# Top-k attention with a feed-forward behind it: weights converted in fewer VectorE operations between search rounds, feed-forward dealt evenly

## The chip, the cores and the metric

One core of a Trainium2 chip runs the whole program. Its engines, as the profile names them: PE (TensorE, matrix products; PEld is its weight load), DVE (VectorE), ACT (ScalarE), POOL (GpSimd) and SP (SyncE, which here only issues transfers); 16 DMA engines move data. The metric is device time in microseconds; lower is better.

## The reference

All inputs are 64-bit floats; the result is 32-bit.

```python
B, H, S, D = 8, 8, 576, 64            # q, k, v: (B, H, S, D)
scores = (1/sqrt(D)) * q @ k.T        # per b, h: 576 x 576
kth = the 32nd largest of each row
scores = where(scores >= kth, scores, -1e9)
attn = exp(scores - max); attn /= sum(attn) + 1e-9
x = (attn @ v) laid out as (B*S, H*D) = (4608, 512)
h = x @ w_in                          # w_in (512, 2048)
g = h - tanh(h)
out = g @ w_out                       # w_out (2048, 512)
```

q, k and v come in as 32-bit floats; w_in and w_out as 64-bit floats, which the kernel turns into 32-bit ones itself.

## The kernel before

**Steps.** The attention is cut into 144 steps: for each of the 8 batch entries 16 main steps (a pair of heads by one of four groups of 128 queries) and 2 remainder steps (64 queries of two pairs of heads), 18 in all. The main loop in `run` is software-pipelined: in its turn n it works on four steps at once. In the order of the code: `weigh(n-2)` (PE transposes of the weights `z` into `zt`, L325, copied out by ACT, L328), `mask(n-1)` (ACT L268, POOL L271), `search(n)` (DVE: the 32 largest of each row by rounds of MAX8 and MATCH_REPLACE8, L227 to L238), some feed-forward, `scores(n+1)` (PE L197, copied to `sc` by ACT L205), the last transpose of `weigh(n-2)` (L331, L332), `expo(n-1)` (ACT L284), feed-forward, `values(n-2)` in every second main step and in remainder steps (PE `av` L355, L363; ACT `xs` L367; POOL `xT` L377), the transposes and copies of q and k (`turn_kq`, L170 to L181) and the loads of a pair of heads, and feed-forward again. Every engine runs its instructions in this order. The scores lie in one PSUM tile (`sc_ps`, one buffer): `scores(n+1)` on PE waits until DVE's L227 and L228 of step n have read it.

**Feed-forward.** A unit is 256 rows of x; there are 18 (two for each batch entry, and one of remainders for every four entries). A unit is 32 items for PE: 16 `ffn_h` (eight matmul records each, L397; after every second one ACT takes tanh, L409, and a copy, L410, and POOL subtracts, L411) and 16 `ffn_o` (four records each, L417). When `values` finishes a unit its items go on the list `work`; `deal(part)` hands out `part` of 4.4 items per step, in three parts of a step (0.5, 0.25, 0.25), for as long as the list holds any. What is left behind the last step runs then.

**Weights.** `convert(j, i)` turns one of 32 pieces of 128 x 512 numbers into 32-bit floats. Its load of 512 KB is issued by SP (L110, tile `raw`). DVE takes the exponent field (L116), ACT scales it (L117), POOL clamps it (L124); DVE takes the upper fraction bits (L119) and adds the lower word (L120), ACT scales (L123); DVE sets the sign (L129), POOL multiplies fraction and power (L132). Turns -1 to 10 of the main loop carry three pieces each, written behind `search`.

The reciprocal of the row sums (`invert`, DVE L303) stands after the first search round of turn n for step n-2; POOL spreads it (L346, tile `rx`) inside `values`.

Of the kernel before, what the change touches and what calls it, by code (L numbers as in the profile page):

```python
# [12 lines left out]
U32 = mybir.dt.uint32  # L13

# [27 lines left out]
def kernel(  # L42
# [41 lines left out]
    hpool = pool("h", 2)  # L84
    thpool = pool("th", 3)
    gpool = pool("g", 6)
# [13 lines left out]
    NW = 512  # L100

    def convert(j, i):

        if j < WJ:
            src, dst = moe_w_in[i * P : (i + 1) * P, j * NW : (j + 1) * NW], w_in[j][:, i, :]
        else:
            r0 = ((j - WJ) * FJ + i) * P
            src, dst = moe_w_out[r0 : r0 + P, :], w_out[j - WJ][:, i, :]
        raw64 = gpool.tile([P, NW, 2], U32, tag="g", name="raw64")
        nc.sync.dma_start(raw64[:].rearrange("p n w -> p (n w)"), src.bitcast(U32))  # L110
        yield
        lo, hi = raw64[:, :, 0], raw64[:, :, 1]
        f = thpool.tile([P, NW], FP32, tag="th", name="f")
        fu = f[:].bitcast(U32)

        nc.vector.tensor_scalar(fu, hi, 20, 0x7FF, ALU.logical_shift_right, ALU.bitwise_and)  # L116
        nc.scalar.activation(f[:], fu, AF.Copy, bias=-896.0 * 2.0**23, scale=2.0**23)  # L117

        nc.vector.tensor_scalar(dst.bitcast(U32), hi, 0x000FFFFF, None, ALU.bitwise_and)  # L119
        nc.vector.scalar_tensor_tensor(  # L120
            out=dst, in0=lo, scalar=2.0**-32, in1=dst.bitcast(U32), op0=ALU.mult, op1=ALU.add
        )
        nc.scalar.activation(dst, dst, AF.Copy, bias=1.0, scale=2.0**-20)  # L123
        nc.gpsimd.tensor_scalar(  # L124
            f[:].bitcast(I32), f[:], 0.0, 255.0 * 2.0**23, ALU.max, ALU.min
        )
        yield

        nc.vector.scalar_tensor_tensor(  # L129
            out=fu, in0=hi, scalar=0x80000000, in1=fu, op0=ALU.bitwise_and, op1=ALU.bitwise_or  # L130
        )
        nc.gpsimd.tensor_tensor(dst, dst, f[:], ALU.mult)  # L132
        yield
# [74 lines left out]
    def search(n, exact):  # L208
# [23 lines left out]
        for i in range(rounds):  # L232
            m8 = slice(8 * i, 8 * i + 8)
            for t in range(2):
                nc.vector.max(m[:, t, m8], last[t] if i == rounds - 1 else cur[t])  # L235
            if i < rounds - 1:
                for t in range(2):
                    nc.vector.match_replace(nxt[t], m[:, t, m8], cur[t], NEG)  # L238
                cur = nxt
            if i == 0:  # L240
                yield
# [57 lines left out]

    def invert(n):  # L300
        g, rd = steps[n], rds.get(n)
        if rd is not None and (g.rem or g.qt % 2):
            nc.vector.reciprocal(rd[:], rd[:])  # L303
# [32 lines left out]
    def values(n):  # L336
# [6 lines left out]
        rd = rds.pop(n)  # L343
        nq = 1 if g.rem else 2
        rx = xpool.tile([P, 2, 2, D], FP32, tag="rx", name="rx")
        nc.gpsimd.tensor_copy(rx[:, 0:nq], rd[:].unsqueeze(3).to_broadcast([P, nq, 2, D]))  # L346
# [19 lines left out]
        xs = xpool.tile([P, 2, N], FP32, tag="xs", name="xs")  # L366
# [46 lines left out]
    def ffn_o(u, i, part):  # L413
# [12 lines left out]
        ot = hpool.tile([P, DM], FP32, tag="ot", name="ot")  # L426
# [4 lines left out]
    def ffn(u):  # L431
        for f in range(CF):
            yield lambda f=f: ffn_h(u, f)
        for i in range(2):
            for part in range(CF // 2):
                yield lambda i=i, part=part: ffn_o(u, i, part)
# [28 lines left out]
    def run(exact):  # L465
        plan()
        NS = len(steps)
        items = len(rests) + len(units)
        share = 1.1 * items * 2 * CF / NS
# [6 lines left out]
        at(-6, lambda: load_kq(*pairs[0]))  # L476
        for i, (b, hp) in enumerate(pairs):
            n = first[b] + 2 * hp
            turn = turn_kq(b, hp)
            at(n - 4, lambda turn=turn: next(turn))  # L480
            at(n - 3, lambda turn=turn: next(turn))
            if i + 1 < len(pairs):
                at(n - 3, lambda i=i: load_kq(*pairs[i + 1]))
            at(n - 2, lambda b=b, hp=hp: load_v(b, hp))
        pieces = [] if exact else [convert(j, i) for j in range(2 * WJ) for i in range(FJ)]
        for i, piece in enumerate(pieces):
            for s in range(3):
                at((i + s) // 3 - 1, lambda piece=piece: next(piece))
        credit = 0.0

        def deal(part):
            nonlocal credit
            credit += part * share
            while work and credit > 0:
                work.pop(0)()
                credit -= 1
            credit = credit if work else min(credit, 0.0)

        for n in range(-6, NS + 2):
            here = lambda i: 0 <= n + i < NS  # L500
            if here(-2):
                w = weigh(n - 2)
                next(w)
            if here(-1):
                mask(n - 1, exact)
            if here(0):
                s = search(n, exact)
                next(s)
                if here(-2):
                    invert(n - 2)  # L510
                next(s, None)
            elif here(-2):
                invert(n - 2)
            deal(0.5)
# [6 lines left out]
            deal(0.25)  # L521
            if here(-2):
                values(n - 2)
            for fn in todo.pop(n, []):
                fn()
            deal(0.25)
        while work:
            work.pop(0)()
# [48 lines left out]
```

## Time and profile before

| | us |
|---|---|
| median of 3 runs | 1871.41 (1869.48 to 1871.91) |
| the profiled execution, its own time | 1873.38 |
| span of that execution, first to last instruction | 1871.6 |

| engine | busy us | share of the span |
|---|---|---|
| PE | 1645.2 | 88% |
| DVE | 1200.5 | 64% |
| ACT | 1066.4 | 57% |
| POOL | 954.0 | 51% |

Busy time is the time in which an engine had an instruction in hand. The shares are averages over a program with stages of different limits, so they are read by stretch. The tables by stretch give for each engine its busy time and in brackets its instructions, then the granted clock of TensorE (1.00 is 2.4 GHz, 0.50 is 1.2 GHz), the busy share of the DMA engines and GB/s. A row of the timeline is: start, duration, engine, line, operation, output<-inputs, count; in square brackets the idle time ahead of it and what ended it.

### The profile page before, as it was taken

The page shows a single profiled execution, that of the slowest core. Times are in us where ns is not written, and L with a number is a line of the kernel's source. Part 1 is how long each engine was busy: PE and PEld are TensorE (multiplying, and loading weights), DVE is VectorE, ACT ScalarE, POOL GpSimd, SP SyncE. Part 2 cuts the span into 40 slices and gives each one's busy share as a digit, 9 for nine tenths or more (in the row PEclk, how much of TensorE's full clock was granted, in tenths as well). Part 3 has the DMA queues.
Part 4 walks back from the last instruction along what each step waited for, and adds up shares of the span by engine and source line. Part 5 has one row for each costly group of instructions (what it writes and reads, how often), then busy time and mean ns, then how long its engine had stood idle before and what let it go on. Part 6 is the DMA issues. An engine that isn't in the chain of part 4 may idle for free.

```text
span 1871.6 us, 25682 instructions
## 1 busy us (share of the span) xinstructions
PE 1645.2 (88%) x8418; PEld 1048.9 (56%) x8418; DVE 1200.5 (64%) x3667; ACT 1066.4 (57%) x2101; POOL 954.0 (51%) x1399
## 2 busy tenths in 40 slices
PE   2233499899989998999999999999989998999998
PEld 1121265657566665757566665757565655656764
DVE  4877886666676667666666665666676667666300
ACT  2444466756575665656565566656565657656511
POOL 2767764545455544646354554545455545555411
PEclk6556699999989998999999999999999999999999
DMA  4232001100120002000111001100120002000000
GB/s 124 87 125 79 34 1 42 46 6 6 26 51 19 7 12 56 21 12 1 41 35 25 7 13 44 38 7 7 32 47 17 7 25 51 6 7 7 6 12 14
DMA packets 102158, 56.28 MB, mean 30 GB/s; under 512 B 85120, under 2 KB 93312, under 8 KB 102016
## 3 DMA queue, kind: packets, MB, share of 16 engines
q1 hardware_dynamic: 102016, 54.56, 10.3%
q8 instruction: 69, 1.13, 0.3%
q14 instruction: 73, 0.60, 0.1%
HBM read 45.09 MB, written 9.44 MB: 29 GB/s over the span
## 4 chain that ended last, share of the span: by engine, by line
PE 79%; POOL 7%; ACT 6%; DVE 5%; issue 2%; SPq 1%; DMA 1%; ACTq 0%; POOLq 0%
PE ops L417 26%; PE hps L397 25%; PE scps L197 9%; PE av L355 8%; PE zt L325 7%; POOL f L124 2%; POOL z L271 2%; ACT z L284 2%; PE av L363 2%; PE zt L331 2%; ACT xs L367 1%; DVE f L129 1%; DVE m L235 1%; ACT sc L205 1%; DVE ab L238 1%
## 5 line engine op out<-in xcount | busy, mean ns | idle before, releaser
L417 PE MATMUL ops<-w_out,g 128*128 128x512 f32 x1152 | 525.8, 595 | 0.0
L271 POOL TENSOR_TENSOR z<-sc,z 128x576 f32<-128x576 f32 x288 | 399.3, 1408 | 235.2 <-ACT z L268 235.2
L397 PE MATMUL hps<-xT,w_in 128*128 128x256 f32 x2048 | 475.2, 383 | 1.0 <-POOL xT L377 1.0
L235 DVE MAX8 m<-ab 128x8 f32<-128x288 f32 (+1 forms) x1152 | 467.0, 447 | 0.0
L227 DVE TENSOR_TENSOR ab<-scps,sc 128x576 f32<-128x576 f32 x144 | 109.0, 757 | 490.0 <-ACT sc L205 437.9
L397 PEld LDWEIGHTS hps<-xT,w_in 128*128 128x128 f32 x2048 | 384.0, 193 | 51.6 <-POOL xT L377 3.1
L238 DVE MATCH_REPLACE8 ab<-m,ab 128x288 f32<-128x288 f32 x864 | 376.2, 443 | 0.0
L197 PE MATMUL scps<-kT,qT 64*128 64x288 f32 (+1 forms) x1280 | 197.9, 464 | 143.7 <-DVE ab L228 143.7
L417 PEld LDWEIGHTS ops<-w_out,g 128*128 128x128 f32 x1152 | 209.8, 193 | 193.6 <-issue 191.3
L205 ACT COPY sc<-scps 128x1152 f32<-128x1152 f32 x144 | 161.3, 1120 | 205.6 <-issue 182.4
L411 POOL TENSOR_TENSOR g<-g,th 128x512 f32<-128x512 f32 x144 | 183.3, 1273 | 182.5 <-ACT g L410 180.3
L197 PEld LDWEIGHTS scps<-kT,qT 64*128 64x128 f32 (+1 forms) x1280 | 106.2, 192 | 234.5 <-issue 94.8
L268 ACT ACTIVATE z<-sc,tbs 128x576 f32<-128x576 f32 x288 | 208.4, 776 | 34.3 <-POOL tbs L255 34.3
L284 ACT ACTIVATE z<-z,nb 128x576 f32<-128x576 f32 x288 | 222.5, 781 | 3.9 <-POOL z L271 3.9
L328 ACT COPY et<-zt 128x512 f32<-128x512 f32 x288 | 156.3, 596 | 92.6 <-PE zt L325 92.6
L325 PE MATMUL zt<-ident,z 128*128 128x128 f32 x1152 | 159.8, 284 | 26.2 <-ACT kT L179 16.7
L325 PEld LDWEIGHTS zt<-ident,z 128*128 128x128 f32 x1152 | 140.1, 146 | 70.1 <-issue 25.3
L298 POOL TENSOR_SCALAR rd<-den 128x2 f32<-128x2 f32 x128 | 28.3, 221 | 259.6 <-ACT z L284 259.5
L355 PE MATMUL av<-et,vb 128*64 128x256 f32 (+1 forms) x1536 | 153.5, 344 | 0.0
L409 ACT ACTIVATE th<-hps 128x512 f32<-128x512 f32 x144 | 85.6, 594 | 111.9 <-PE hps L397 107.7
L355 PEld LDWEIGHTS av<-et,vb 128*64 128x64 f32 x1536 | 88.1, 141 | 68.9 <-ACT e L332 23.1
L367 ACT COPY xs<-av 128x512 f32<-128x512 f32 (+1 forms) x80 | 43.5, 544 | 139.8 <-PE av L363 139.8
(62 smaller groups left out, 1487.9 us busy)
## 6 DMA issues: line engine op xcount, KB each, us to landing
kin<-in_k_dram SPq DMA_DIRECT2D x64, 128.0 KB, 2.5
qin<-in_q_dram SPq DMA_DIRECT2D x64, 128.0 KB, 2.5
vb<-in_v_dram SPq DMA_DIRECT2D x64, 128.0 KB, 2.3
raw<-in_moe_w_in_dram SPq DMA_DIRECT2D x16, 512.0 KB, 6.0
raw<-in_moe_w_out_dram SPq DMA_DIRECT2D x16, 512.0 KB, 3.2
out_dram<-ot SPq DMA_DIRECT2D x32, 256.0 KB, 2.3
kin<-in_k_dram SPq DMA_DIRECT2D x64, 16.0 KB, 2.3
qin<-in_q_dram SPq DMA_DIRECT2D x64, 16.0 KB, 2.3
```

Of the source, the lines that this page charges most:

```text
L197: nc.tensor.matmul(ps[rows, t, s, 0:S2], qT[g.b, g.hp + i][half(t), qs], kT[g.b, g.hp + i][half(t), ks], start=True, stop=True,)
L205: nc.scalar.copy(sc[:], ps[:, :, :, 0:S2])
L235: nc.vector.max(m[:, t, m8], last[t] if i == rounds - 1 else cur[t])
L238: nc.vector.match_replace(nxt[t], m[:, t, m8], cur[t], NEG)
L268: nc.scalar.activation(zv[:, t, :], scf[:, t, :], AF.Relu, bias=tbs[:, t, n : n + 1], scale=-BIG)
L271: nc.gpsimd.tensor_tensor(zv[:, t, :], scf[:, t, :], zv[:, t, :], ALU.subtract)
L284: nc.scalar.activation(x["zv"][:, t, :], x["zv"][:, t, :], AF.Exp, bias=x["nb"][:, t : t + 1], scale=scale, accum_out=den[:, t : t + 1],)
L325: nc.tensor.transpose(zt[:, c * P : (c + 1) * P], z[:, m0 + c * P : m0 + (c + 1) * P], ident[:])
L355: nc.tensor.matmul(av[half(t), 0, cols], vb[g.b, hp][:, t, c, :] if c < J else vr[g.b, hp][rows, :], et[:, t, c, cols] if c < J else e4[ro ...
L397: nc.tensor.matmul(ps[:, f % 2, :], w_in[j][:, c, fo : fo + P], u.xT[:, c, :], start=(c == 0), stop=(c == CD - 1),)
L411: nc.gpsimd.tensor_tensor(g, g, th[:], ALU.subtract)
L417: nc.tensor.matmul(cur[u][:], u.g[f // FJ][:, f % FJ, i * P : (i + 1) * P], w_out[f // FJ][:, f % FJ, :], start=(f == 0), stop=(f == CF - 1),)
```

## The change

- `convert` loads each piece twice, on the ACT queue instead of SP's: once as it is, and once from three bytes further on (tile `shifted`), so that one 32-bit word holds the upper 28 fraction bits. DVE is left with three operations (exponent, fraction, sign), POOL with one (the product); the clamp is two ACT operations, the second in place of POOL's. Three pieces are loaded at the start, and a later one when the piece three ahead of it is done.
- The pieces are dealt to the gaps between the four search rounds of turns 0 to 16: one in each of turns 0 to 8, four in turn 9, three in 10 to 15, the last in 16.
- `deal` spreads the items in the list evenly over the turns until the next unit arrives, in parts 0.4, 0.2, 0.2, 0.2; an item also waits until the weights that it reads are converted. `values` and the turning of q and k now have a part between them.
- From turn 17 on the reciprocal stands at the end of a turn, behind `expo`, for step n-1, and POOL's spread at the start of the next. Before that both stay with the search.
- The turning of q and k, and their loads, come one step later; the loop starts at -4 instead of -6.
- Buffers: `raw` and `shifted` have pools of three, `g` 4 instead of 6, `th` 4 instead of 3 (the output tile `ot` is now one of them), `xs` one instead of two.

```diff
-    hpool = pool("h", 2)
-    thpool = pool("th", 3)
-    gpool = pool("g", 6)
+    thpool = pool("th", 4)
+    gpool = pool("g", 4)
+    rawpool = pool("raw", 3)
+    shpool = pool("shifted", 3)
...
-        raw64 = gpool.tile([P, NW, 2], U32, tag="g", name="raw64")
-        nc.sync.dma_start(raw64[:].rearrange("p n w -> p (n w)"), src.bitcast(U32))
+        raw = rawpool.tile([P, NW, 2], U32, tag="raw", name="raw")
+        nc.scalar.dma_start(raw[:].rearrange("p n w -> p (n w)"), src.bitcast(U32))
+        shifted = shpool.tile([P, NW, 2], U32, tag="shifted", name="shifted")
+        nc.scalar.dma_start(
+            shifted[:].rearrange("p n w -> p (n w)").bitcast(U8)[:, 0 : 8 * NW - 4],
+            src.bitcast(U8)[:, 3 : 8 * NW - 1],
+        )
         yield
-        lo, hi = raw64[:, :, 0], raw64[:, :, 1]
+        hi = raw[:, :, 1]
         f = thpool.tile([P, NW], FP32, tag="th", name="f")
         fu = f[:].bitcast(U32)
 
+
         nc.vector.tensor_scalar(fu, hi, 20, 0x7FF, ALU.logical_shift_right, ALU.bitwise_and)
-        nc.scalar.activation(f[:], fu, AF.Copy, bias=-896.0 * 2.0**23, scale=2.0**23)
-
-        nc.vector.tensor_scalar(dst.bitcast(U32), hi, 0x000FFFFF, None, ALU.bitwise_and)
-        nc.vector.scalar_tensor_tensor(
-            out=dst, in0=lo, scalar=2.0**-32, in1=dst.bitcast(U32), op0=ALU.mult, op1=ALU.add
+        nc.scalar.activation(f[:], fu, AF.Relu, bias=e1151[:], scale=-(2.0**23))
+        nc.scalar.activation(f[:].bitcast(I32), f[:], AF.Relu, bias=e255[:], scale=-1.0)
+
+        nc.vector.tensor_scalar(
+            dst.bitcast(U32), shifted[:, :, 0], 0x0FFFFFFF, None, ALU.bitwise_and
         )
-        nc.scalar.activation(dst, dst, AF.Copy, bias=1.0, scale=2.0**-20)
-        nc.gpsimd.tensor_scalar(
-            f[:].bitcast(I32), f[:], 0.0, 255.0 * 2.0**23, ALU.max, ALU.min
-        )
+        nc.scalar.activation(dst, dst.bitcast(U32), AF.Copy, bias=1.0, scale=2.0**-28)
         yield
 
         nc.vector.scalar_tensor_tensor(
...
-            if i == 0:
-                yield
+            between(i)
 
...
     def invert(n):
-        g, rd = steps[n], rds.get(n)
-        if rd is not None and (g.rem or g.qt % 2):
-            nc.vector.reciprocal(rd[:], rd[:])
+        if last_of_pair(n):
+            nc.vector.reciprocal(rds[n][:], rds[n][:])
+
+    rxs = {}
+
+    def spread(n):
+
+        if last_of_pair(n):
+            rd = rds.pop(n)
+            nq = rd.shape[1]
+            rx = rxs[n] = xpool.tile([P, 2, 2, D], FP32, tag="rx", name="rx")
+            nc.gpsimd.tensor_copy(rx[:, 0:nq], rd[:].unsqueeze(3).to_broadcast([P, nq, 2, D]))
 
...
         for f in range(CF):
-            yield lambda f=f: ffn_h(u, f)
+            yield CD * (f // FJ + 1), lambda f=f: ffn_h(u, f)
         for i in range(2):
             for part in range(CF // 2):
-                yield lambda i=i, part=part: ffn_o(u, i, part)
+                yield CD * (WJ + part // 2 + 1), lambda i=i, part=part: ffn_o(u, i, part)
 
...
             turn = turn_kq(b, hp)
-            at(n - 4, lambda turn=turn: next(turn))
             at(n - 3, lambda turn=turn: next(turn))
+            at(n - 2, lambda turn=turn: next(turn))
             if i + 1 < len(pairs):
-                at(n - 3, lambda i=i: load_kq(*pairs[i + 1]))
-            at(n - 2, lambda b=b, hp=hp: load_v(b, hp))
+                at(n - 2, lambda i=i: load_kq(*pairs[i + 1]))
+            at(n - 1, lambda b=b, hp=hp: load_v(b, hp))
+
         pieces = [] if exact else [convert(j, i) for j in range(2 * WJ) for i in range(FJ)]
-        for i, piece in enumerate(pieces):
-            for s in range(3):
-                at((i + s) // 3 - 1, lambda piece=piece: next(piece))
-        credit = 0.0
+        many = {9: 4} | {n: 1 for n in range(9)} | {n: 3 for n in range(10, 17)}
+        EARLY = 0 if exact else 17
+        parts, started = {}, 0
+        for m in range(EARLY):
+            mine = range(started, min(started + many[m], len(pieces)))
+            started = mine.stop
+            seq = [(1, i) for i in mine[:1]]
+            for i in mine[1:]:
+                seq += [(1, i), (2, i - 1)]
+            seq += [(2, i) for i in mine[-1:]]
+            for x, (part, i) in enumerate(seq):
+                parts.setdefault((m, 3 * x // max(len(seq) - 1, 1)), []).append((part, i))
+        for piece in pieces[:3]:
+            next(piece)
+        converted = [0 if pieces else 2 * WJ * FJ]
+
+        def between(i):
+            for part, k in parts.pop((n, i), []):
+                next(pieces[k])
+                if part == 2:
+                    converted[0] = k + 1
+                    if k + 3 < len(pieces):
+                        next(pieces[k + 3])
+            if i == 0 and 0 <= n - 2 and n < EARLY:
+                invert(n - 2)
+
+        credit, share = 0.0, [0.0]
 
         def deal(part):
+
             nonlocal credit
-            credit += part * share
-            while work and credit > 0:
-                work.pop(0)()
+            credit += part * share[0]
+            while work and credit > 0 and work[0][0] <= converted[0]:
+                work.pop(0)[1]()
                 credit -= 1
-            credit = credit if work else min(credit, 0.0)
-
-        for n in range(-6, NS + 2):
+            credit = min(credit, 1.0)
+
+        for n in range(-4, NS + 2):
             here = lambda i: 0 <= n + i < NS
+            more = min([m + 2 for m in done if m + 2 >= n], default=n)
+            share[0] = len(work) / (more - n + 1)
             if here(-2):
+                if n >= EARLY:
+                    spread(n - 2)
                 w = weigh(n - 2)
                 next(w)
             if here(-1):
                 mask(n - 1, exact)
             if here(0):
-                s = search(n, exact)
-                next(s)
-                if here(-2):
-                    invert(n - 2)
-                next(s, None)
-            elif here(-2):
-                invert(n - 2)
-            deal(0.5)
+                search(n, exact, between)
+            if here(-2) and n < EARLY:
+                spread(n - 2)
+            deal(0.4)
             if here(1):
                 scores(n + 1)
             if here(-2):
                 next(w)
             if here(-1):
                 expo(n - 1)
-            deal(0.25)
+                if n + 1 >= EARLY:
+                    invert(n - 1)
+            deal(0.2)
             if here(-2):
                 values(n - 2)
+            deal(0.2)
             for fn in todo.pop(n, []):
                 fn()
-            deal(0.25)
-        while work:
-            work.pop(0)()
+            deal(0.2)
+        for _, fn in work:
+            fn()
+        work.clear()
         return NS
 
```

How the change moves instructions is shown at three places, by rows of the order of one engine's instructions (line, operation, output<-inputs, shape; a number behind a name is a buffer's).

DVE in the search of step 1, from the first round's MAX on; before, where the search (L235 MAX, L238) is whole and three pieces follow it:

```order
L235 MAX m<-ab 128x8 x2
L238 MATCH_REPLACE ab<-m,ab 128x288 x2
L235 MAX m<-ab 128x8 x2
L129 SCALAR_TENSOR_TENSOR f<-raw_298,f 128x512
L116 TENSOR_SCALAR f<-raw_307 128x512
L119 TENSOR_SCALAR w_in_111<-raw_307 128x512
L120 SCALAR_TENSOR_TENSOR w_in_111<-raw_307,w_in_111 128x512
L129 SCALAR_TENSOR_TENSOR f<-raw_307,f 128x512
```

and after, where the search's lines are L245 and L248:

```order
L245 MAX m<-ab 128x8 x2
L248 MATCH_REPLACE ab<-m,ab 128x288 x2
L129 TENSOR_SCALAR f<-raw 128x512
L133 TENSOR_SCALAR w_in_113<-shifted 128x512
L245 MAX m<-ab 128x8 x2
```

The three pieces behind a search, four operations each, became one piece inside it: two operations behind the first round and its sign (L139, not in these rows) behind the last.

ACT in the same stretch, some steps on; before, around the copy of the scores (L205):

```order
L328 COPY et<-zt 128x4x128 x2
L268 ACTIVATE z<-sc,tbs 128x576 x2
L205 COPY sc<-scps 128x1152
L332 COPY e_644<-zt 128x128
L284 ACTIVATE z,den<-z,nb 128x576 x2
```

and after, around the same copy (L215):

```order
L349 COPY et<-zt 128x4x128 x2
L277 ACTIVATE z<-sc,tbs 128x576 x2
L130 ACTIVATE f<-f,e_121 128x512
L131 ACTIVATE f<-f,e_123 128x512
L136 ACTIVATE w_in_114<-w_in_114 128x512
L117 DMA raw<-in_moe_w_in_dram 128x1024
L119 DMA shifted<-in_moe_w_in_dram 128x4092
L215 COPY sc<-scps 128x1152
L353 COPY e_537<-zt 128x128
L293 ACTIVATE z,den<-z,nb 128x576 x2
```

Three conversion operations and two transfers, which refill the buffers of the piece just done, now stand ahead of the copy.

PE where the second unit's feed-forward begins; before:

```order
L355 MATMUL av<-et,vb 64x256 x8
L355 MATMUL av<-e_2056,vr 64x256 x2
L363 MATMUL av<-ident,rx 128x128 x2
L170 MATMUL kqps<-ident,qin 128x128 x4
L174 MATMUL kqps<-ident,qin 128x64
L397 MATMUL hps<-xT,w_in_110 128x256 x8
L325 MATMUL zt<-ident,z 128x128 x8
```

and after:

```order
L374 MATMUL av<-et,vb 64x256 x8
L374 MATMUL av<-e_2060,vr 64x256 x2
L382 MATMUL av<-ident,rx 128x128 x2
L436 MATMUL ops<-w_out_120,g 128x512 x2
L180 MATMUL kqps<-ident,kin 128x128 x4
L184 MATMUL kqps<-ident,kin 128x64
L436 MATMUL ops<-w_out_120,g 128x512 x2
L346 MATMUL zt<-ident,z 128x128 x8
L416 MATMUL hps<-xT,w_in_113 128x256 x4
```

The last items of the unit before now stand on both sides of the turning of k, and the new unit's first item behind the next step's transposes.

## Rows read from the trace of the kernel before

**Rows 1.** The page: busy time by engine, and TensorE's granted clock in 40 slices.
```profile
PE 1645.2 (88%) x8418; PEld 1048.9 (56%) x8418; DVE 1200.5 (64%) x3667; ACT 1066.4 (57%) x2101; POOL 954.0 (51%) x1399
PEclk6556699999989998999999999999999999999999
```
**Rows 2.** Busy time by stretch: conversion, steps 18 to 143, and what follows.
```profile
29.70:235.16 205.46, 67.24 (x316) 40.03 (x316) 168.11 (x365) 89.31 (x164) 145.22 (x132) 0.60 0.22 76
316.72:1740.30 1423.58, 1367.84 (x7182) 873.76 (x7181) 958.84 (x3083) 883.55 (x1751) 726.45 (x1151) 0.98 0.09 23
1740.30:1871.60 131.30, 123.93 (x475) 80.59 (x474) 9.87 (x29) 33.50 (x66) 31.80 (x37) 0.98 0.04 11
```
**Rows 3.** Timeline of step 4's search and the conversions behind it, DVE and POOL.
```profile
111.83 0.74 DVE L227 TENSOR_TENSOR ab<-scps,sc 128x576 f32<-128x576 f32 x1
...
119.34 0.67 DVE L129 SCALAR_TENSOR_TENSOR f<-raw,f 128x512 uint32<-128x512 uint32 x1
...
120.27 0.42 DVE L119 TENSOR_SCALAR w_in<-raw 128x512 uint32<-128x512 uint32 x1
...
124.18 0.69 DVE L129 SCALAR_TENSOR_TENSOR f<-raw,f 128x512 uint32<-128x512 uint32 x1 [1.82 <-POOL f L124]
...
125.03 1.31 POOL L132 TENSOR_TENSOR w_in<-w_in,f 128x512 f32<-128x512 f32 x1 [0.88 <-DVE f L129]
125.13 1.50 DVE L119 TENSOR_SCALAR w_in<-raw 128x512 uint32<-128x512 uint32 x1
...
131.81 0.74 DVE L227 TENSOR_TENSOR ab<-scps,sc 128x576 f32<-128x576 f32 x1
```
**Rows 4.** Groups by line and form, 0 to 215 us: conversion on POOL and ACT.
```profile
L124 POOL TENSOR_SCALAR f<-f 128x512 int32<-128x512 f32 x29 | 61.1, 2107 | 25.0 <-ACT f L117 24.4
L117 ACT ACTIVATE f<-f 128x512 f32<-128x512 uint32 x29 | 18.3, 631 | 59.8 <-DVE f L116 59.8
```
**Rows 5.** The page's costliest groups: POOL's and ACT's work in a step.
```profile
L271 POOL TENSOR_TENSOR z<-sc,z 128x576 f32<-128x576 f32 x288 | 399.3, 1408 | 235.2 <-ACT z L268 235.2
...
L205 ACT COPY sc<-scps 128x1152 f32<-128x1152 f32 x144 | 161.3, 1120 | 205.6 <-issue 182.4
...
L268 ACT ACTIVATE z<-sc,tbs 128x576 f32<-128x576 f32 x288 | 208.4, 776 | 34.3 <-POOL tbs L255 34.3
```
**Rows 6.** The chain that ended last: start, length; `av`, and sixteen items.
```profile
136.06 4.19 PE av L355 x20
...
1781.94 27.47 PE ops L417 x64
```
**Rows 7.** Tile `raw`: how long SP takes to issue its loads, ns min/median/max.
```profile
L110 SPq DMA_DIRECT2D raw<-in_moe_w_in_dram x16: 327/430/585, 19.2 to 105.2; - x16
```
**Rows 8.** Busy time by stretch: q and k loads alone, then weight loads.
```profile
5.00:10.00 5.00, 2.47 (x10) 1.46 (x8) 0.00 (x0) 2.08 (x6) 0.00 (x0) 1.00 0.51 115
...
25.00:30.00 5.00, 0.00 (x0) 0.00 (x0) 3.64 (x5) 0.98 (x3) 4.12 (x3) 0.50 0.99 378
```
**Rows 9.** Timeline of PE: scores of steps 120 to 125, feed-forward in all of them.
```profile
1485.12 1.24 PE L197 MATMUL scps<-kT,qT 64*128 64x288 f32 x8
...
1498.08 1.24 PE L197 MATMUL scps<-kT,qT 64*128 64x288 f32 x8
...
1507.28 1.24 PE L197 MATMUL scps<-kT,qT 64*128 64x288 f32 x8
...
1519.29 1.24 PE L197 MATMUL scps<-kT,qT 64*128 64x288 f32 x8
...
1531.01 1.24 PE L197 MATMUL scps<-kT,qT 64*128 64x288 f32 x8
...
1544.16 1.24 PE L197 MATMUL scps<-kT,qT 64*128 64x288 f32 x8
```
**Rows 10.** Timeline of PE: scores of steps 19 and 20, the list empty.
```profile
326.27 1.75 PE L197 MATMUL scps<-kT,qT 64*128 64x288 f32 x8
...
334.52 2.29 PE L197 MATMUL scps<-kT,qT 64*128 64x288 f32 x8
```

More of the change, by code (lines that the diff above doesn't have):

```diff
@@ L13 @@
 U32 = mybir.dt.uint32
+U8 = mybir.dt.uint8
 NEG = -3.0e38
@@ L100 @@
     NW = 512
+    e1151 = consts.tile([P, 1], FP32, name="e1151")
+    nc.gpsimd.memset(e1151[:], 1151.0 * 2.0**23)
+    e255 = consts.tile([P, 1], FP32, name="e255")
+    nc.gpsimd.memset(e255[:], 255.0 * 2.0**23)
     def convert(j, i):
@@ L206, in scores, with search @@
         st[n] = dict(sc=sc, ps=ps)
-    def search(n, exact):
+    def search(n, exact, between):
         x = st[n]
@@ L298, in expo, with last_of_pair @@
         nc.gpsimd.tensor_scalar(rd[:, 0 if g.rem else g.qt % 2, :], den[:], EPS, None, ALU.add)
+    def last_of_pair(n):
+        return steps[n].rem or steps[n].qt % 2 == 1
     def invert(n):
-        g, rd = steps[n], rds.get(n)
-        if rd is not None and (g.rem or g.qt % 2):
-            nc.vector.reciprocal(rd[:], rd[:])
+        if last_of_pair(n):
[7 more added lines that the diff above has]
+            nc.gpsimd.tensor_copy(rx[:, 0:nq], rd[:].unsqueeze(3).to_broadcast([P, nq, 2, D]))
     ets = {}
@@ L342, in values @@
         ets.pop(n - 1, None)
-        rd = rds.pop(n)
+        rx = rxs.pop(n)
         nq = 1 if g.rem else 2
-        rx = xpool.tile([P, 2, 2, D], FP32, tag="rx", name="rx")
-        nc.gpsimd.tensor_copy(rx[:, 0:nq], rd[:].unsqueeze(3).to_broadcast([P, nq, 2, D]))
         w = nq * P
@@ L365, in values @@
             )
-        xs = xpool.tile([P, 2, N], FP32, tag="xs", name="xs")
+        xs = xrpool.tile([P, 2, N], FP32, tag="xs", name="xs")
         nc.scalar.copy(xs[:, :, 0:w], av[:, :, 0:w])
@@ L425, in ffn_o @@
             return
-        ot = hpool.tile([P, DM], FP32, tag="ot", name="ot")
+        ot = thpool.tile([P, DM], FP32, tag="th", name="ot")
         nc.scalar.copy(ot[:], cur[u][:])
@@ L467, in run @@
         NS = len(steps)
-        items = len(rests) + len(units)
-        share = 1.1 * items * 2 * CF / NS
         todo = {}
@@ L475, in run @@
         pairs = [(b, hp) for b in range(B) for hp in range(NHP)]
-        at(-6, lambda: load_kq(*pairs[0]))
+        at(-4, lambda: load_kq(*pairs[0]))
         for i, (b, hp) in enumerate(pairs):
```

## The prediction, made before the kernel was run

> **What bounds the kernel now.** I read the page first, and it deceives: PE is busy for 88% of the span, which looks like a kernel at its bound. The granted clock in 40 slices [rows 1] shows the exception: in the first four or five slices it lies between 0.5 and 0.7, so PE is starved there. The table by stretch [rows 2] then cuts the span in three. While weights are converted, from search 0 at 29.70 to search 10 at 235.16, PE is busy for 67 of 205 us at a granted clock of 0.60, and DVE for 168. From the scores of step 18 to those of step 143 PE is busy for 1368 of 1424 us, and DVE has 465 us to spare. Behind the scores of step 143 stand 131 us of almost nothing but feed-forward. So DVE sets the pace of the first stretch, PE that of the others, and the busy share of PE hides what its bubbles cost.
>
> The timeline of a conversion turn [rows 3] shows why the first stretch is slow: search 4 starts at 111.83, its conversions at 119.34 (7.5 us of search), the next search at 131.81: a turn of 20.0 us, 12.5 of it for three pieces, 4.2 each. DVE's four operations are held up by POOL: once it waits 1.82 us for POOL's clamp, which takes 2.1 us for each piece [rows 4], and the fraction operation, 0.42 us when POOL is idle, takes 1.50 and ends just behind POOL's product [rows 3].
>
> **Part A, up to the scores of step 18 (before: 316.7).** The new turn, on the path search, loads, scores, next search. DVE: 7.5 for the search, two operations of 0.42 and a sign operation of 0.69 make 9.0 [rows 3]. In between POOL subtracts twice; a DVE operation beside it can be held up, so I add 0.5 us and keep 0 to 2.8 (none, or both of them whole; two of L271 are 2.8, [rows 5]). The operation removed took 0.7 to 1.6 us and POOL's clamp is gone, so nothing else on DVE waits for POOL's long operation.
>
> New is a wait on ACT: the load that refills `raw` waits for the sign operation, the last of the search, and the copy of the next scores (1.12 us, [rows 5]) is queued behind it, so DVE's next search waits for both. ACT has not issued a load here; on SP one takes 0.33 to 0.59 us [rows 7], so two take 0.9 (0 to 1.2: if ACT issues while it computes, they cost nothing). That makes 9.0 + 0.5 + 0.9 + 1.1 + 0.1 = 11.6 us for a turn with one piece. In turns with `av` ACT's own order is longer: the copy of `av` waits for PE, whose 20 products take 4.2 us at the low clock [rows 6], and behind it come the transposes' copies, the mask's two operations of 0.78 [rows 5] and two for the exponent (0.63, [rows 4]), for which the sign operation waits. I count 13 to 15.6 for these, and 12.5 as the mean of turns 0 to 8: 9 x 12.5 = 112.
>
> Turns 10 to 15 have three pieces: DVE 7.5 + 3 x 1.53 = 12.1, plus some 3 for POOL's products and subtractions beside it; then 0.9 of loads, a tanh and a copy that now stand ahead of the scores' copy, together about as long as it, and 1.2 for that: 18.5 a turn, 111 in all. ACT alone has 14 us of work in such a turn and up to 3 of issuing, so it is close to being the bound itself. Turn 9 with four pieces gets 19, turn 16 with one 13, and 8 more pass until the scores of step 18. The first search starts at about 17: 13 us after the loads of q and k as now, or up to 20 because six weight loads (3 MB) stand beside them, which at 378 GB/s [rows 8] are 8 us. Sum: 17 + 112 + 19 + 111 + 13 + 8 = 280, bounds 245 and 320. Of 576 items 24 are then done, against 32 before.
>
> The Trainium skill (SBUF — State Buffer, Who interferes with whom) calls the port that VectorE shares with GpSimd an exclusive lock, held for a whole instruction. The 1.50 us of [rows 3] agree. By it every turn could pay the whole 2.8 us, and part A would end at 280 + 17 x 2.3 = 319; I stay nearer to the low end because in most turns the subtractions begin only when the two operations behind round 0 are over.
>
> **Part B, scores of step 18 to scores of step 143 (before: 1423.6).** One item costs 27.5/16 = 1.72 us [rows 6]. Steps with the list full [rows 9] take 13.0 (remainder, 5 items), 9.2 (4 items), 12.0 (`av`, 4), 11.7 (k turned, 5) and 13.15 (`av`, q turned, 4). With 4 items in each, a batch entry has four pairs of 12.0 + 9.2, four of 13.15 + 10.0, and two remainder steps of 11.2: 199.8 us for 72 items, so 186 for 64. The 125 steps at that rate are 7 x 186 x 125/126 = 1292 with 445 items. Before has 478 items in them: 1292 + 33 x 1.72 = 1349, and the real stretch is 75 us longer. Those 75 us are steps in which the list is empty (19 takes 8.3 us without one, [rows 10]; there are ten such) and the steps in which a new unit arrives, where the first half of the turn has nothing to fill PE's waits. The even dealing takes both away: three or four items in nearly every step, and the last ones of a unit kept for the arrival of the next. It holds 505 items here: 1292 + 60 x 1.72 = 1395. I add 15 for thinner cover (where a part has no item, PE waits ahead of `av` for ACT, about the 1.1 us of the scores' copy, [rows 5]), so 1410; bounds 1385 (the part between `values` and the turning covers another wait) and 1470 (nothing gained from evenness).
>
> The reciprocal at the end of a turn waits for the exponential of step n-1, which ACT reaches some 2.9 us after the scores' copy, and the next search is queued behind it. DVE has 465/125 = 3.7 us to spare per step [rows 2], so it costs nothing while PE is the bound; without that cover it is 2.9 us in every second step. In return POOL's spread is ready ahead of `av`. q and k turn one step later, with as much time between load and use as before. SP loses the weight loads, behind which q, k and v loads used to stand.
>
> **Part C, behind the scores of step 143 (before: 131.3).** Before leaves 66 items there, after 47: 131.3 - 19 x 1.72 = 98.6, say 99. It can't be under 84: the last search, mask, exponential and `av` take some 21, the last unit 55, the end 7.
>
> **Sum.** 280 + 1410 + 99 = 1789; the profiled execution's own time is 1.8 above its span, so 1791, against 1873.4. The median of the runs is 0.1% under that execution; I say 1790, 4.3% less than before.
>
> **Rivals.**
>
> *The early part gains nothing.* ACT or the lock bounds the turns with pieces: ACT's 14 us of work plus 6 issues of 0.6 plus its waits for PE make 21 to 22 a turn, and the turns with one piece 14.5. Part A then ends at 17 + 130 + 22 + 130 + 14 + 8 = 321, the time is about 1831. For it: ACT becomes the fullest engine there. Against it: it still shares the turn with DVE, which before needed 20.
>
> *Evenness gains nothing.* PE's in-order waits are what cost, not the empty list; with three items a step instead of four or five each wait shows. The loss stays 75 us: 280 + 1470 + 99, so 1851. Against it: the steps of four items in [rows 9] are already as thin as the new ones.
>
> *Slower: the shifted loads land late.* They start three bytes off a word and hold 4092 bytes; no row shows such a load. Plain weight loads reach 378 GB/s at 0.99 busy, so 1.4 us for 512 KB; the slowest kind here, q and k in runs of 256 bytes, 115 at 0.51, so 2.3 us [rows 8]. Both are hidden in a turn of 12 us. The loads decide once a piece takes over 80/29 = 2.8 us more than its share of 8.3 in part A, so 11 us; a shifted load would have to run at 55 GB/s, a quarter of the slowest row. At 13 us a piece part A ends at 17 + 29 x 13 + 21 = 415 and the time is 1926.
>
> The Trainium skill (DMA: Bandwidth & Descriptors, How a descriptor splits into AXI transactions) says that a run which doesn't start on a 256-byte boundary is read from the boundary below it. By that a shifted run costs no more than a plain one, and this rival would not happen; no run here shows it.
>
> **How the numbers follow.** The forecast, 1755 to 1825, has 0.74; no early gain (1831) 0.09; no gain from evenness (1851) 0.07; slower 0.07; 0.03 lies below 1755, if issuing on ACT and the lock cost nothing. The range 1750 to 1840 takes in the forecast and the first rival. A measurement of this kernel tells about 0.2% from no change. Faster 0.90, same 0.02 (where two rivals meet), slower 0.08.
>
> **What would show it.** Searches 0 to 8 start 11.5 to 13 us apart and those of turns 10 to 15 some 18.5; the scores of step 18 start near 280; ACT's copy of the scores waits behind the loads. From there a batch entry takes 187 to 190 us instead of 199, no step is without an item, and some 100 us stand behind the last scores. The prediction is wrong if DVE waits for transfers in the first 280 us, if DVE's first operation of a search waits for the exponential instead of for the scores, or if PE's idle time per step in part B is what it was.

## The result, and the profile after

The changed kernel takes 1765.85 us (1765.66 to 1765.94) against 1870.45 for the kernel before in the same comparison: a ratio of 0.944, 95% interval 0.9425 to 0.9457, so 5.6% less. 1790 was predicted.

The page of the changed kernel, as [rows 1], with the chain that ended last (shares of the span by engine; a q stands for the engine's sequencer, which issues transfers and takes the waits) below:

```profile
PE 1628.9 (92%) x8418; PEld 1041.7 (59%) x8418; DVE 1159.9 (66%) x3635; ACT 1086.1 (62%) x2133; POOL 893.2 (51%) x1369
PEclk9777789999999999999999999999999999999999
PE 86%; DVE 7%; ACT 4%; issue 1%; ACTq 1%; POOL 0%; DMA 0%; SPq 0%; DVEq 0%; POOLq 0%
```

Its tables by stretch, columns as in [rows 2]: conversion (search 0 to scores of step 18), scores of step 18 to those of step 143, and the rest:

```profile
17.85:269.45 251.60, 142.44 (x708) 92.48 (x707) 194.53 (x524) 165.15 (x306) 135.69 (x175) 0.77 0.40 136
269.45:1665.91 1396.46, 1389.77 (x7359) 891.68 (x7358) 956.42 (x3083) 890.23 (x1769) 732.40 (x1154) 1.00 0.09 24
1665.91:1764.00 98.09, 91.08 (x335) 53.98 (x334) 8.97 (x30) 26.20 (x51) 24.30 (x33) 0.99 0.04 12
```

Part A ends at 269.5 us (316.7 before, 280 predicted), part B takes 1396.5 (1423.6; 1410), part C 98.1 (131.3; 99). In the middle row PE is idle for 6.7 us, in that of [rows 2] for 55.7, though it has 7359 records to run instead of 7182. All three terms came out within 4%. Part B did so with half of its reason missing, as six of the experiments show.

A conversion turn of the changed kernel, that of search 3 (DVE, ACT and ACT's queue; columns as in [rows 3]):

```profile
51.53 0.76 DVE L237 TENSOR_TENSOR ab<-scps,sc 128x576 f32<-128x576 f32 x1 [2.11 <-ACT sc L215]
...
55.16 0.41 DVE L129 TENSOR_SCALAR f<-raw 128x512 uint32<-128x512 uint32 x1
...
55.49 0.42 DVE L133 TENSOR_SCALAR w_in<-shifted 128x512 uint32<-128x512 uint32 x1
...
59.79 0.67 DVE L139 SCALAR_TENSOR_TENSOR f<-raw,f 128x512 uint32<-128x512 uint32 x1
...
60.49 0.34 ACTq L117 DMA_DIRECT2D raw<-in_moe_w_in_dram  x1
...
60.87 0.44 ACTq L119 DMA_DIRECT2D shifted<-in_moe_w_in_dram  x1
...
61.35 1.12 ACT L215 COPY sc<-scps 128x1152 f32<-128x1152 f32 x1 [1.90 <-DVE f L139]
...
62.58 0.76 DVE L237 TENSOR_TENSOR ab<-scps,sc 128x576 f32<-128x576 f32 x1 [2.12 <-ACT sc L215]
```

A turn with one piece is 11.05 us, against 20.0 with three in [rows 3]: DVE's work ends at 60.46, two loads are issued, the scores are copied, and 2.1 us after its last operation DVE starts the next search.

The scores of steps 120 to 125, as in [rows 9]:

```profile
1382.18 1.24 PE L207 MATMUL scps<-kT,qT 64*128 64x288 f32 x8
1393.41 1.24 PE L207 MATMUL scps<-kT,qT 64*128 64x288 f32 x8
1400.90 1.24 PE L207 MATMUL scps<-kT,qT 64*128 64x288 f32 x8
1411.21 1.24 PE L207 MATMUL scps<-kT,qT 64*128 64x288 f32 x8
1418.69 1.24 PE L207 MATMUL scps<-kT,qT 64*128 64x288 f32 x8
1431.00 1.24 PE L207 MATMUL scps<-kT,qT 64*128 64x288 f32 x8
```

The step with `av` from 1400.90 takes 10.31 us with three items; that of [rows 9] took 12.0 with four. The difference of 1.7 is one item. No step of part B is without an item (ten were), and a batch entry with 64 items takes 185.8 us, where 186 was worked out from the fullest steps.

### The profile page after: what moved, and what is told of

Its sections match the earlier page's. It is cut to its first block, busy times and chain, and to the rows that moved or that the text cites. A ratio compares the mean times of both kernels' runs of the same rounds, so it can differ in the third digit from the quotient of the medians.

```text
span 1764.0 us, 25564 instructions
## 1 busy us (share of the span) xinstructions
PE 1628.9 (92%) x8418; PEld 1041.7 (59%) x8418; DVE 1159.9 (66%) x3635; ACT 1086.1 (62%) x2133; POOL 893.2 (51%) x1369
## 3 DMA queue, kind: packets, MB, share of 16 engines
q8 instruction: 68, 1.11, 0.2%
## 4 chain that ended last, share of the span: by engine, by line
PE 86%; DVE 7%; ACT 4%; issue 1%; ACTq 1%; POOL 0%; DMA 0%; SPq 0%; DVEq 0%; POOLq 0%
PE ops L436 28%; PE hps L416 27%; PE av L374 10%; PE scps L207 8%; PE zt L346 7%; DVE m L245 2%; PE zt L352 2%; PE av L382 2%; DVE ab L248 2%; DVE f L139 1%; PE kqps L180 1%; ACT sc L215 1%; ACT z L277 1%; PE kqps L184 1%; ACTq L119 0%
## 5 line engine op out<-in xcount | busy, mean ns | idle before, releaser
L245 DVE MAX8 m<-ab 128x8 f32<-128x288 f32 (+1 forms) x1152 | 467.9, 448 | 0.0
L248 DVE MATCH_REPLACE8 ab<-m,ab 128x288 f32<-128x288 f32 x864 | 375.8, 443 | 0.0
L215 ACT COPY sc<-scps 128x1152 f32<-128x1152 f32 x144 | 160.3, 1113 | 116.3 <-ACT z L277 46.5
L314 DVE RECIPROCAL rd<-rd 128x4 f32<-128x4 f32 x64 | 11.3, 177 | 310.2 <-POOL rd L307 310.1
L207 PE MATMUL scps<-kT,qT 64*128 64x288 f32 (+1 forms) x1280 | 188.1, 447 | 8.4 <-DVE ab L238 8.0
L207 PEld LDWEIGHTS scps<-kT,qT 64*128 64x128 f32 (+1 forms) x1280 | 101.0, 184 | 100.5 <-issue 33.9
L374 PE MATMUL av<-et,vb 128*64 128x256 f32 (+1 forms) x1536 | 148.0, 336 | 0.0
L240 DVE MAX8 ab<-ab 128x8 f32<-128x288 f32 x288 | 116.8, 447 | 0.0
```

The costliest lines, as they stand in the source:

```text
L207: nc.tensor.matmul(ps[rows, t, s, 0:S2], qT[g.b, g.hp + i][half(t), qs], kT[g.b, g.hp + i][half(t), ks], start=True, stop=True,)
L215: nc.scalar.copy(sc[:], ps[:, :, :, 0:S2])
L374: nc.tensor.matmul(av[half(t), 0, cols], vb[g.b, hp][:, t, c, :] if c < J else vr[g.b, hp][rows, :], et[:, t, c, cols] if c < J else e4[ro ...
```

## Experiments

Each ratio is against runs of the kernel before on the same chip. In the tables A, B and C are the three parts of the profiled execution, as above.

**One part of the change at a time.** Dealing alone (e1) is the kernel before with

```
+            share[0] = len(work) / (more - n + 1)
...
-            deal(0.5)
+            deal(0.4)
```

and the rest of the four parts; conversion alone (e2) and the two undo runs below are the changed kernel with the old lines of the diff put back (buffers stay as changed).

> The kernel before with the even dealing alone (shares, four parts, the part between values and the turning); conversion, reciprocal, q and k stay. Theory (the three gains add up, and B and C belong to the dealing): part A stays at about 317, part B takes the 1396 and part C the 98 us that the changed kernel took: 317 + 1396 + 98 + 2 = 1813, 0.969 of before. Rival (the other moves carry part of B): B stays above 1410 and the time above 1827. Rival (evenness gains nothing): 1870.

> The changed kernel with the old dealing (4.4 items a turn in three parts), the old places of the reciprocal and its spread, and the old turns for q and k: the new conversion alone. Theory: part A takes the 269 us of the changed kernel (317 before), B and C stay at 1424 and 131: 1824, 0.975 of before; with e1 the two savings add up to the whole of 104.6 us. Rival (a faster part A only brings the empty list earlier, and part of it is given back): 1840 or more.

In the changed kernel the reciprocal and its spread were put back (e3), then the turning of q and k (e4):

```
             if i == 0 and 0 <= n - 2:
                 invert(n - 2)
...
             if here(-2):
+                spread(n - 2)
                 values(n - 2)
```

> The changed kernel with the reciprocal behind the first round of the search in every turn, and POOL's spread in front of av, as before. Theory: PE is the bound from step 18 on, and DVE has 3.5 us to spare in a step, so neither place costs anything: 1766, within 0.2%. Rival 1 (the wait for the exponential at the end of a turn costs): faster, by up to 2.9 us in every second step that isn't covered. Rival 2 (av waits for the spread in the old place): slower, by 0.5 us in each of 80 av, 40 us.

> The changed kernel with the turning of q and k, and the loads of q, k and v, one step earlier, as before. Theory: the same work on PE and ACT, one turn away from its use either way: 1766, within 0.2%, with the first search some 2 us later at most, as the loop has two more turns ahead of it with little in them. Rival (the later turning takes a wait away): slower by 0.5% or more, with PE's idle time in front of the scores.

| | time us | ratio to before, 95% | A | B | C |
|---|---|---|---|---|---|
| before | 1870.45 | 1 | 316.7 | 1423.6 | 131.3 |
| changed | 1765.85 | 0.9425 to 0.9457 | 269.5 | 1396.5 | 98.1 |
| e1 dealing alone | 1878.43 | 1.0021 to 1.0043 | 315.2 | 1459.7 | 98.1 |
| e2 conversion alone | 1850.10 | 0.9868 to 0.9906 | 288.1 | 1423.7 | 131.4 |
| e3 old reciprocal | 1849.19 | 0.9864 to 0.9899 | 279.7 | 1466.0 | 98.2 |
| e4 old turning | 1769.72 | 0.9439 to 0.9470 | 271.8 | 1397.7 | 98.2 |

The parts are to be read with the items that they hold: 24, 505 and 47 in A, B and C with the even dealing (changed, e1, e3, e4), 32, 478 and 66 in before, 29, 481 and 66 in e2. So e1's longer B is no loss of 36 us: it holds 27 more items, 46 us at 1.72 each.

Even dealing by itself saves nothing (0.3% slower), conversion by itself saves 1.1%, and putting the reciprocal and its spread back costs 83 us: of the three parts that were taken out of the changed kernel one at a time (e3, e4 and, below, the dealing in e5) the move that "costs nothing" is worth the most. The place of q and k is worth 3.9 us at most, the intervals overlap, and the first search of e4 starts at 21.7 us instead of 17.9. The old conversion was not put back into the changed kernel, and no run parts the conversion's own moves (fewer operations, ACT's queue, pieces between the rounds, new pools). PE's waits for rx (from 330 to 1700 us; engine, tile, line, releaser; us in total, times, longest) in before, and its longest kind of wait in the changed kernel:

```profile
PE av L363 <- POOL rx L346: 26.4, 17, 2.1
```

```profile
PE zt L346 <- ACT qT L189: 2.4, 5, 0.5
```

In e1 it is 51.0 us at 36 `av`, in e3 49.3 at 35. The timeline of e3 shows where the spread is held up:

```profile
1468.75 0.17 DVE L314 RECIPROCAL rd<-rd 128x4 f32<-128x4 f32 x1
...
1471.17 2.78 POOL L280 TENSOR_TENSOR z<-sc,z 128x576 f32<-128x576 f32 x2 [0.41 <-ACT z L277]
...
1474.94 0.22 POOL L307 TENSOR_SCALAR rd<-den 128x2 f32<-128x2 f32 x1 [0.78 <-ACT z L293]
1475.09 0.65 PE L374 MATMUL av<-e,vr 64*64 64x256 f32 x4
...
1475.89 1.26 POOL L430 TENSOR_TENSOR g<-g,th 128x512 f32<-128x512 f32 x1 [0.74 <-ACT g L429]
...
1477.10 0.39 POOL L324 COPY rx<-rd 128x256 f32<-128x256 f32 x1
...
1477.55 0.44 PE L382 MATMUL av<-ident,rx 128*128 128x128 f32 x2 [1.81 <-POOL rx L324]
```

The reciprocal is there at 1468.9, 8.2 us before the spread. What keeps the spread is POOL's queue: ahead of it stand the mask's subtractions, the row sum of the *next* step (which waits for ACT's exponential), and a feed-forward subtraction. PE's products are over by 1475.74, and its queue stands for 1.81 us. In the changed kernel the spread for the `av` of the same step runs at the turn's start, 5.7 us ahead of its reader:

```profile
1400.78 0.40 POOL L324 COPY rx<-rd 128x256 f32<-128x256 f32 x1
...
1406.51 0.44 PE L382 MATMUL av<-ident,rx 128*128 128x128 f32 x2
```

**The spread's place, and the dealing with it.** e5 is the changed kernel with the old dealing. e6 takes the reciprocal back into the search and moves the spread behind the search only; e10 makes this one edit in the kernel before:

```
+            if here(-2):
+                spread(n - 2)
             deal(0.5)
```

> The changed kernel with the old dealing (4.4 items a turn, parts 0.5, 0.25, 0.25, none between values and the turning); the reciprocal and its spread stay at their new places. It completes a table of two by two with e2 and e3 (both near 1850) and the changed kernel (1766). Theory (the spread, which in the old place stands in POOL's queue behind the sum of the next step's exponential and a feed-forward subtraction, is what PE waits for, 26 us of direct waits with the old dealing against 49 with the even one; and the empty list costs besides): 1850 - 26 - some 5 behind them = 1820, so evenness is worth some 54 us once that wait is gone. Rival 1 (evenness is worth nothing, the whole gain of B and C is the spread's): 1766 to 1775. Rival 2 (each helps only where the other is in place): 1845 or more.

> The changed kernel with the reciprocal back behind the first round of the search in all turns, and POOL's spread right behind the search, ahead of the next step's row sum and of the feed-forward's subtraction in POOL's queue (as the changed kernel has it in turns 0 to 16). Theory (only the spread's place in POOL's queue matters, not where DVE takes the reciprocal): within 0.5% of the changed kernel, 1766 to 1775. Rival 1 (the reciprocal in the search is itself what comes late): 1845 as in e3. Rival 2 (the spread waits there behind POOL's two subtractions of the mask, and av in steps whose part holds no item still waits): between, 1790 to 1820.

> The kernel before with one edit: POOL's spread of the reciprocals stands right behind the search instead of in front of av, so ahead of the next row sum in POOL's queue; the reciprocal stays. Theory (the spread's place alone takes PE's waits away, whatever the dealing): B loses the 24.5 us that lie between e2's and e5's, part A stays at 317 since DVE's conversion sets it: 1846, 0.986 of before. Rival (the place only pays where the new conversion has emptied POOL's queue): within 0.4% of before.

| | time us | ratio to before, 95% | A | B | C |
|---|---|---|---|---|---|
| e5 old dealing | 1812.64 | 0.9655 to 0.9701 | 280.7 | 1399.2 | 130.9 |
| e6 spread behind search | 1767.17 | 0.9426 to 0.9460 | 267.8 | 1396.5 | 99.3 |
| e10 spread alone, on before | 1845.19 | 0.9849 to 0.9882 | 315.6 | 1396.9 | 130.9 |

e6 equals the changed kernel, and differs from e3 in the spread alone. So it is the spread's place in POOL's queue that pays; where DVE takes the reciprocal makes no difference. Two lines moved in the kernel before (e10; `spread` as in the change's diff) save 25 us, all in part B, and leave 7.6 us of waits for rx. With the new conversion the four corners are:

| | spread in front of `av` | spread moved |
|---|---|---|
| old dealing | 1850 (e2) | 1813 (e5) |
| even dealing | 1849 (e3) | 1766 |

Evenness is worth 1 us in the left column, less than the scatter of these runs (1845 to 1853), and 47 in the right; e2 has the old turning besides, some 4 us (e4), which leaves this as it is. PE's idle time in B says the same: with the spread in front of `av` evenness leaves it at 53.1 us (e2) and 61.6 (e3), with the spread moved it falls from 29.5 (e5) to 6.7. Part B of e5 and of e3:

```profile
280.72:1679.94 1399.22, 1369.73 (x7198) 872.74 (x7198) 954.78 (x3077) 878.55 (x1752) 722.04 (x1149) 0.98 0.09 23
279.65:1745.62 1465.97, 1404.41 (x7359) 900.29 (x7358) 956.85 (x3076) 890.58 (x1769) 733.15 (x1155) 0.99 0.09 23
```

e3 has the same 7359 records as the changed kernel. Against e5 the changed kernel gains busy time too: 24 more items, 41 us at 1.72 each, add only 20 to PE's 1369.7, at a granted clock of 1.00 instead of 0.98. Why the waits for rx double under even dealing (17 to 36 from before to e1) no run shows by itself, but the traces point to it: the spread that ends the wait runs directly behind a feed-forward subtraction of POOL at 4 of before's 17 waits and at 19 of e1's 36. An item dealt behind `expo` puts its subtraction ahead of the spread.

**What sets the early turns.** e7 issues the refill loads behind the copy of the scores; e8 also puts all signs behind the search; e9 is e7 with two pieces in each of turns 0 to 15. e12 is the changed kernel with no item before turn 17.

```
-                    if k + 3 < len(pieces):
-                        next(pieces[k + 3])
+                    refill.extend(pieces[k + 3 : k + 4])
...
                 scores(n + 1)
+            while refill:
+                next(refill.pop(0))
```

e8, besides:

```
+            for i in mine:
+                parts.setdefault((m, 0), []).append((1, i))
+                parts.setdefault((m, 3), []).append((2, i))
```

e9, besides e7's lines, and e12, in the changed kernel:

```
+        many = {n: 2 for n in range(16)} | {16: 0}
```

```
+            share[0] = len(work) / (more - n + 1) if n >= EARLY else 0.0
```

> The changed kernel with the two refill loads of a piece issued on ACT behind the copy of the next scores instead of ahead of it. Theory (from the sign operation's end to the copy's start ACT takes 0.9 us, for issuing two loads, and DVE's next search waits for that copy): 0.9 us less in each of the 15 turns that refill, 13 us: 1753. Rival (ACT issues the loads at the end of a turn whose length is set by its own work or by PE, and they come back elsewhere in the turn): within 4 us of 1766.

> As e7, and in turns with several pieces all exponent and fraction operations stand behind the first round of the search and all sign operations behind the last. In the changed kernel DVE waits up to 7 us in the middle of such a search for ACT's clamp, which stands behind copies that wait for PE. Theory (the wait shortens, as the search goes on while ACT catches up): turns 10 to 15 take 17 us instead of 19.6, 15 us less than e7: 1738. Rival (ACT and PE set those turns, whatever DVE does): as e7, within 4 us.

> As e7, with two pieces in each of turns 0 to 15 instead of one, four and three. Theory (DVE sets the turns without feed-forward, 8.9 to 9.9 us with one piece, and ACT and PE those with it, 15 to 20 with three): a second piece adds its 1.5 us of DVE to the first nine turns and takes some 4 us of ACT's and DVE's work from turns 9 to 15: 9 x 11 + 7 x 14 instead of 9 x 9.5 + 7 x 19, 20 us less: 1727. Rival 1 (the first turns are held by loads or by ACT too, and get as much longer as the later ones get shorter): within 4 us of e7. Rival 2 (turns 9 to 15 are set by PE's transposes and items at the low clock, not by conversion): 1755 or more.

> The changed kernel with no feed-forward item ahead of turn 17, so that turns 9 to 16 hold attention and conversion alone; the 24 items left out there come later. The scores of step 16 less those of step 10 are 119.6 us in the changed kernel (six turns with three pieces, 19.9 each). Theory (PE's items stand ahead of the transposes of z, ACT's copies wait for them, and the conversion's operations, for which DVE waits, stand behind those copies): the six turns take 17 us each, 102, and the time is 1766 - 18 + 24 x 1.72 = 1789. Rival (ACT's own work sets those turns): 115 to 120 for the six, and 1803 or more.

Mean turns by the starts of DVE's searches:

| | time us | ratio to before, 95% | turns 0 to 8 | turn 9 | turns 10 to 15 | A |
|---|---|---|---|---|---|---|
| changed | 1765.85 | 0.9425 to 0.9457 | 11.21 | 17.74 | 18.67 | 269.5 |
| e7 loads behind scores | 1746.35 | 0.9314 to 0.9347 | 9.75 | 18.87 | 17.55 | 250.5 |
| e8 signs last | 1748.21 | 0.9322 to 0.9356 | 9.76 | 19.68 | 17.36 | 252.8 |
| e9 two a turn | 1741.89 | 0.9299 to 0.9330 | 12.22 | 12.72 | 13.86 | 244.1 |
| e12 no early items | 1789.10 | 0.9540 to 0.9577 | 11.20 | 17.74 | 16.28 | 260.4 (5 items) |

e7 saves 19 us of part A where 13 were expected: 1.5 us in each of the first nine turns, more than the 0.9 of issuing. The end of e7's turn of search 3 shows that the copy no longer waits for the sign operation either, but runs beside it, and DVE waits for 0.24 us instead of 2.1:

```profile
56.38 1.36 DVE L139 SCALAR_TENSOR_TENSOR f<-raw,f 128x512 uint32<-128x512 uint32 x1
56.77 1.10 ACT L215 COPY sc<-scps 128x1152 f32<-128x1152 f32 x1
57.77 0.34 ACTq L117 DMA_DIRECT2D raw<-in_moe_w_in_dram  x1
57.97 0.76 DVE L237 TENSOR_TENSOR ab<-scps,sc 128x576 f32<-128x576 f32 x1 [0.24 <-ACT sc L215]
```

e8 changes nothing beyond it, so DVE's wait in the middle of the search isn't what sets those turns. e9 is the fastest kernel here, 6.9% under before, yet it saves 4.5 us on e7 where 20 were expected (part A is 6.4 shorter; the intervals of the ratios overlap), which is nearer to its rival 1: turns 10 to 15 fall by 3.7 us each, not 5, and turns 0 to 8 rise by 2.5, not 1.5. e12 hits both its numbers (six turns 101.4 us from scores to scores, expected 102; time 1789): the items lengthen the turns with pieces. One way is that ACT's copies wait for PE and the conversion stands behind those copies. Two rows of the changed kernel, search 11's turn, show this path from PE over ACT to DVE; the third is the same sign operation in e12:

```profile
161.98 0.60 ACT L428 ACTIVATE th<-hps 128x512 f32<-128x512 f32 x1 [5.29 <-PE hps L416]
...
167.57 1.35 DVE L139 SCALAR_TENSOR_TENSOR f<-raw,f 128x512 uint32<-128x512 uint32 x1 [7.07 <-ACT f L131]
```

```profile
160.88 1.35 DVE L139 SCALAR_TENSOR_TENSOR f<-raw,f 128x512 uint32<-128x512 uint32 x1 [1.34 <-ACT f L131]
```

The 18 items dealt in between lengthen the six turns by 119.6 - 101.4 = 18.2 us, 1.0 each, and an item later costs 1.72, so doing them early still pays. How much of the 18.2 is waiting for PE stays open: e12 leaves out ACT's tanh and copies of these items as well, 9.5 us of its work in the six turns, while ACT's idle time that PE ended falls from 12.5 to 6.6.

**The byte offset.** e11 reads the second copy from the first byte instead of the fourth.

> The changed kernel with the second load of each piece taken from the piece's first byte instead of its fourth, same length (the weights' fractions are then not those of the reference): what the byte offset costs. Theory (transfers are hidden, DVE waits for none of them): 1766 within 0.2%, and the landing of the second load falls from 4.6 us towards the first one's 3.7. Rival (the offset slows the shared DMA engines): faster by 0.5% or more.

1765.55 us (0.9422 to 0.9454), the changed kernel's time. The page's rows for the second load into `w_in` (KB, median us to landing), in the changed kernel and in e11:

```profile
shifted<-in_moe_w_in_dram ACTq DMA_DIRECT2D x16, 511.5 KB, 4.6
```

```profile
shifted<-in_moe_w_in_dram ACTq DMA_DIRECT2D x16, 511.5 KB, 4.7
```

The offset costs nothing. The expectation that an aligned second load would land like the first (3.7 us) was wrong: it lands later with either start, so the 0.9 us are not the offset's.

## Why the prediction came out near, and which step failed

**Bound.** Right: PE was starved in part A and bound in part B; the chain of the changed kernel is 86% PE.

**Part A, 280 against 269.5.** The path held (search, loads, copy of the scores), the term for turns 0 to 8 was too large: 11.2 us each instead of 12.5, which is 11 us; the other differences cancel. The single terms stand in the timeline above: DVE 8.93 from the search's start to the sign's end (9.0 predicted, without the 0.5 for the shared port), 0.89 of issuing (0.9), 1.2 for the copy. Turns with `av` took 11.0 to 12.1, where 13 to 15.6 were counted. Turns 10 to 15 came at 18.7 (18.5), turn 9 at 17.7 (19). But conversion alone ends part A at 288.1, with a first search that starts 3.7 us later: some 10 us of the 47 are the spread's (e3, 279.7), and as many the dealing's (e5, 280.7, with 29 items done by then instead of 24), neither of which the sum priced. The spread counts here because in turns 0 to 16 only the reciprocal stays where it was: the kernel before has the spread inside `values`, the changed one right behind the search. On the shared port: the Trainium skill (SBUF — State Buffer, Who interferes with whom) speaks of an exclusive lock, and long cases are there, as the sign operation of 1.35 us beside a POOL subtraction shows against 0.67 alone; but of the 27 conversion operations of turns 0 to 8 only three were long (0.75, 1.11 and 1.35 us, each beside POOL's subtraction), 0.16 us a turn where 0.5 was added, and the 319 us that would follow from paying it every time did not come.

**Part B, 1410 against 1396.5: the step that failed.** "The even dealing takes both away" gave evenness the whole 75 us that before loses against the full rate, and the reciprocal's move "costs nothing", its return one sentence on a spread that is ready. The runs show the reverse order: evenness without the move 1 us (e2 to e3), the move without evenness 37.5 (e2 to e5, some 4 of it the turning) or 25 (e10), both 84. The rate of 186 us for a batch entry was right because full steps in [rows 9] were taken as the goal, and the changed kernel reaches it (185.8). Of the 75 us, 49 were PE's idle time (55.7 less 6.7). Some 25 were its busy time: 27 more items should have added 46 us to before's 1367.8 and added 22. In before the granted clock is below 0.99 in 14 steps of B, 13 of which have no item or come directly behind a step without one; in the changed kernel it is in none. What was missing is a row that before's own trace holds and that was not read: PE's 26.4 us of waits at the last products of `av`, released by POOL's rx. The rival "evenness gains nothing" had put B at 1470 and the time at 1851; e3, 1466 and 1849, is that rival, and only the edit priced at nothing kept it from happening. The 15 us for thin cover named ACT's copy as what PE would wait for; the wait there was POOL's spread, and the move took it away, so nothing of the 15 was needed.

**Part C, 99 against 98.1.** Right, by the count of items (47).

**The reciprocal at the end of a turn** costs nothing, as predicted: e6, without it, has the same time, though DVE now waits there for most of what it has to spare (groups by line and form, 270 to 1665 us; busy, mean ns, idle ahead of it and what ended it):

```profile
L314 DVE RECIPROCAL rd<-rd 128x4 f32<-128x4 f32 x55 | 9.8, 178 | 302.0 <-POOL rd L307 302.0
```

**The slower rival** (late shifted loads) did not come: the offset costs nothing (e11), and DVE waited for no load. The Trainium skill (DMA: Bandwidth & Descriptors, How a descriptor splits into AXI transactions) has a run that starts off a 256-byte boundary read from the boundary below it. By that these runs cost no more with the offset, and the 4.6 and 4.7 us agree.

## What to carry to other kernels

Before an operation's move is priced at nothing, list what stands ahead of it in its own engine's queue in the old place, and look up who waits for its output; a small copy behind another step's wait can hold the bound engine. Gains of two edits need not add: evenness was worth 1 us or 47, depending on where the spread stood, so both orders of undoing are to be run, and parts of a run are compared with the work that they hold. And a load's issue belongs behind the copy that the next step waits for, which here took 19 us off with a few lines.

## What was not expected of the hardware

- ACT issues a load in 0.33 to 0.45 us (62 of 64 in the changed kernel; the others 0.57 and 0.63), and its next copy starts only behind both: 0.89 us from the end of the sign operation to the copy in the turn of search 3.
- Two loads of 512 KB issued right after each other by ACT land 3.7 and 4.6 us after their issue, with or without the byte offset; with twice as many in a turn (e9) these are 4.5 and 5.7.
- PE's same 7359 records of part B keep it busy for 1389.8 us in the changed kernel (granted clock 1.00) and 1404.4 in e3 (0.99): where PE waits more, its busy time is longer too.
